# A three-stage kernel in fp32 split into halves: VectorE's and ScalarE's order in nine Strassen pairs of the channel mix is worked out by host code

## The chip, the cores and the metric

The kernel runs on one core of a Trainium2 chip. Times are device microseconds (us) of one execution. Beside the plain executions one was taken by the hardware profiler, and all rows below come from it. A core has TensorE (PE) for matmuls, VectorE (DVE), ScalarE (ACT), GpSimd (POOL, idle here) and SyncE (SP), which issues the transfers. Each engine has an instruction list of its own, and semaphores tie the lists together; in the trace every engine but PE's weight loads goes through its list in order.

## The reference

Three stages follow each other. The inputs are fp32.

```
scores = z @ z.T / S;  x = u * (relu(scores)**2 @ v)            # attention, 4 x 3072 x 256
x_prev = x shifted by one token
xk = mu_k*x + (1-mu_k)*x_prev;  xr = mu_r*x + (1-mu_r)*x_prev   # channel mix, 12288 tokens
x = sigmoid(xr @ w_r) * (relu(xk @ w_k)**2 @ w_v)               # 256 -> 1024 -> 256
out = relu(x @ w_in)**2 @ w_out                                 # MLP, 256 -> 2048 -> 256
```

## The kernel before

**Numbers.** A product of fp32 matrices is made of three matmuls of rounded numbers: an operand is cast to a high half (`hi`), and `lo = x - hi` holds the rest; `hi*hi`, `lo*hi` and `hi*lo` are added in PSUM. So each operand that comes out of a stage costs one cast and one subtraction. All matmuls of the mix and the MLP have 512 columns.

**Tiling.** The 12288 tokens are 24 blocks of 512. In the channel mix, blocks 0 to 5 go through plain matmuls. Blocks 6 to 23 go in nine pairs (`s` = 3 to 11) through a Strassen-Winograd form with seven products in place of eight; the MLP then takes the twelve pairs in the same form (`s` = 12 to 23). The change concerns the nine pairs of the mix.

**A round.** A pair of the mix has four rounds `(s, i)`, i = 0 to 3, each for two of the eight slices of the hidden layer. A round is written as units: `p0` to `p6` are the seven products (three matmuls each) into four PSUM banks, and `d0` to `d7` are the second layer's matmuls (three each) on the hidden tiles of the round before, in the order p0 d0 p1 d1 ... p6 d6 d7. Rounds 1 and 2 have two more units, `r0` and `r1`, of six matmuls each: the gate `xr @ w_r` of one block, into bank 1, which becomes `sig`. So a pair has 4 x 45 + 24 = 204 matmuls, and the nine have 1836.

**What VectorE and ScalarE do in a round.** ACT copies bank 0 (`p`, L916). DVE adds the banks up: `su` (bank 1), `sv` (bank 2), `s` for the hidden quarters 22, 12 and 21 (all L920). ACT makes relu and square (L925, L929), then a cast makes the high half (`hhi`, ACT L934 or DVE L936) and DVE the low half (`hlo`, L940). Bank 1 may be written again only when `su` has been made from it, bank 2 only after `sv`.

**What else they do in a pair.** The next pair's operands are prepared meanwhile: blocks of x are loaded (`load_x`, one buffer, x<-xT), blended on ACT and DVE (L191, L194) into the pair's `x2` tile, summed (`sums`, L851 to L855), and split into seven operands (`op_hi` L783, `op_lo` L787), which lie in nine buffers. The gate's operand `xr` is blended and split too (L798, L802). At a pair's end the two accumulators per block are multiplied by `sig` (`gate_v2`, L1029) and stored. Pieces of the MLP's weights are loaded and split (L711, L720).

**What sets the order.** All is under a manual schedule: an engine's order is the order in which the Python code emits. In the pairs of the mix a fixed table (`mix_tasks`) hangs each extra step on a unit, as `at(1, "p1", blend_r, n1, 0)`, and the steps of a round itself hang on units in one long if-chain. Scratch tiles come from rings in turn: `a` (4 tiles, p, v and the blends), `t` (6 tiles, the sums and hidden quarters), `h` (6 pairs of halves).

Of the kernel before, what the change touches and what calls it, by code (L numbers as in the profile page):

```python
# [23 lines left out]
def tile_relu2_attention__rwkv_channel_mix__relu2_mlp(  # L24
# [63 lines left out]

    def split(hi, lo, src, on_act=False):
        if on_act:  # L90
            nc.scalar.copy(hi, src)
        else:
            nc.vector.tensor_copy(hi, src)
        nc.vector.tensor_tensor(out=lo, in0=src, in1=hi, op=ALU.subtract)
# [93 lines left out]
    def blend(n, which, c, xm=None):  # L188
        t = x_t[n]
        m = el.tile([P, T], F32, tag="a", name="m")  # L190
        nc.scalar.activation(out=m, in_=t[:, c, 0:T], func=AF.Copy, scale=om[:, which, c:c + 1])  # L191
        if xm is None:
            xm = el.tile([P, T], F32, tag="a", name="xm")
        nc.vector.scalar_tensor_tensor(out=xm, in0=t[:, c, 1:], scalar=mu[:, which, c:c + 1], in1=m,  # L194
                                       op0=ALU.mult, op1=ALU.add)
        return xm
# [436 lines left out]
    def gate_v(n, d):  # L633
        t = hp.tile([P, T], F32, tag="t", name="xo", bufs=6)
        nc.vector.tensor_tensor(out=t, in0=acc_v[n][d], in1=sig.pop((n, d)), op=ALU.mult)
# [4 lines left out]
    def gate_r(n, d, xr, bank=None):  # L640
        ps = up(lambda h, c, f: wr[:, h, c, f * P:(f + 1) * P], xr, d, bank)
# [4 lines left out]
    def channel_mix():  # L646
# [25 lines left out]
        for f, *tasks in ((0, (stage_x, s, 1, 0), (wk_sums, 0, 0)), (1, (stage_x, s, 1, 1), (load_x, n0), (wk_sums, 0, 1)),  # L672
# [4 lines left out]
                           (load_x, n0 + 1), (load_wk, 1))):  # L677
# [25 lines left out]
    x2_raw, x2_tmp, ops, win, wout = {}, {}, {}, {}, {}  # L703
# [31 lines left out]
    def wk_split(h, g):  # L735
        i = 2 * h + g
        if h == 0:
# [6 lines left out]
        split(*ws[i], wk_total[h][1][:, g], True)  # L744
# [20 lines left out]
    def stage_x(s, b, c):  # L765
        if s not in x2_raw:
            x2_raw[s] = hp.tile([P, ND, 2 * T], F32, tag="x2", name="x2")
        blend(2 * s + b, 0, c, x2_raw[s][:, c, b * T:(b + 1) * T])
# [4 lines left out]
    def op_src(s, j):  # L773
        src = x2_raw[s].rearrange("x c (b t) -> x c b t", b=2)
        return (src[:, 0, 0], src[:, 0, 1], x2_tmp[s][:, 0] if s in x2_tmp else None, x2_tmp[s][:, 1], src[:, 1, 0],
                src[:, 1, 1], src[:, 1, 0])[j]

    def op_hi(s, j):
# [4 lines left out]
        nc.scalar.copy(ops[s, j][0], op_src(s, j))  # L783
# [10 lines left out]
    def blend_r(n, c):  # L794
        mixing[n, c] = blend(n, 1, c)

    def r_hi(n, c):
        nc.scalar.copy(xr_tile()[:, 0, c], mixing[n, c])  # L798
# [75 lines left out]
    def mlp():  # L874
# [39 lines left out]
        def first_sum(g):  # L914
            tmp[g, "p1"] = t = brief("p1")
            nc.scalar.copy(t, banks[g, 0])  # L916

        def add(g, to, bank, of):
            tmp[g, to] = t = (brief if to == "v" else scratch)("s" + to)
            nc.vector.tensor_tensor(out=t, in0=banks[g, bank], in1=tmp[g, of], op=ALU.add)  # L920

        def relu(g, c):
            if c == "11":
                tmp[g, c] = scratch("s11")
# [6 lines left out]
        def high(g, c):  # L931
            hi, lo = gt[g, c] = parts(hp, "h", 6)
            if c in ("22", "11") or (c == "12" and g[0] < NPAIR):
                nc.scalar.copy(hi, tmp[g, c])  # L934
            else:
                nc.vector.tensor_copy(hi, tmp[g, c])  # L936
# [60 lines left out]
        def side(g, stage):  # L997

            p, i = g
            if p < NPAIR:  # L1000
                return
# [30 lines left out]
        split_at = [(s, i) for s in range(PLAIN + 1, NPAIR) for i in (0, 1)][:12]  # L1032
        load_at = {(PLAIN, 3): 0, split_at[3]: 1, split_at[5]: 2, split_at[9]: 3}

        def mix_tasks(s):
            nxt, (n0, n1), (m0, m1) = s + 1, (2 * s, 2 * s + 1), (2 * s + 2, 2 * s + 3)
            more = nxt < NPAIR
            todo = {}

            def at(i, u, *a):  # L1040
                todo.setdefault((i, u), []).append(a)

            if s == PLAIN:
                at(0, "p1", op_hi, s, 4)
                at(0, "p1", op_lo, s, 4)
                at(0, "p1", op_hi, s, 5)
                at(0, "p1", sums, s, 2)
                at(0, "p1", op_lo, s, 5)
                at(0, "p2", op_hi, s, 6)
                at(0, "p2", op_lo, s, 6)  # L1050
                at(0, "p5", wk_sums, 1, 0)
                at(0, "p6", wk_sums, 1, 1)
                at(1, "p3", wk_split, 1, 0)
                at(1, "p4", wk_split, 1, 1)
            else:
                at(0, "p1", op_hi, s, 6)
                at(0, "p2", op_lo, s, 6)
            at(1, "p1", blend_r, n1, 0)
            at(1, "p2", blend_r, n1, 1)
            at(1, "r1", r_hi, n1, 0)  # L1060
            at(1, "r1", r_hi, n1, 1)
            at(1, "p5", r_lo, n1, 0)
            at(1, "p6", r_lo, n1, 1)
            if more:
                at(1, "p2", load_x, m1)
                at(1, "p6", stage_x, nxt, 1, 0)
                at(1, "d7", stage_x, nxt, 1, 1)
                at(1, "d7", load_x, m0)
                at(2, "p2", stage_x, nxt, 0, 0)
                at(2, "p3", stage_x, nxt, 0, 1)  # L1070
                at(2, "p5", blend_r, m0, 0)
                at(2, "p6", r_hi, m0, 0)
                at(2, "d7", r_lo, m0, 0)
                at(3, "p1", blend_r, m0, 1)
                at(3, "p1", load_x, m1)
                at(3, "p2", r_hi, m0, 1)
                at(3, "p3", r_lo, m0, 1)
            else:
# [161 lines left out]
```

## Time and profile before

| | |
|---|---|
| median of 3 runs | 2550.35 us (2545.96 to 2552.53) |
| profiled execution | 2551.01 us; its span, first to last instruction, 2549.1 us |
| PE busy | 2479.4 us, 97% of the span, 14745 matmuls |
| DVE, ACT busy | 2075.5 us (81%), 1830.8 us (72%) |
| mean granted clock of PE | 0.998 of full speed |

A busy PE in such a page is not PE at its peak, since matmuls overlap and their ends are modelled: a matmul of 512 columns shows some 389 ns, and the next may start earlier. What PE loses is therefore read from how far apart matmuls start.

### The profile page before, as it was taken

To read this page: it belongs to the slowest core of one execution; us is meant where nothing else is said; L and a number is where in the kernel's file an instruction comes from. 1 tells how busy PE (TensorE), PEld (TensorE's weight loads), DVE (VectorE), ACT (ScalarE), POOL (GpSimd) and SP (SyncE) were. 2 spreads that over 40 slices of the span, in tenths; PEclk is the share of its full clock that TensorE was granted. 3 is DMA by queue.
4 is the path that set the end of the run, shared out by engine and by line. 5 is a ranking of instruction groups with operands and counts; after the bars stand their busy time and mean duration, and the time that the engine had idled before them with its cause. 6 is when DMAs were issued, how large, how long until landed. Compare 5 with 4: busy or idle time off the path is not lost.

```text
span 2549.1 us, 39363 instructions
## 1 busy us (share of the span) xinstructions
PE 2479.4 (97%) x14745; PEld 2026.2 (79%) x14745; DVE 2075.5 (81%) x3431; ACT 1830.8 (72%) x3239; POOL 0.7 (0%) x6
## 2 busy tenths in 40 slices
PE   9999999999999999988888889999999999999999
PEld 6888898888888888766767667888888888888887
DVE  8998999889899868877788777877777777777776
ACT  8867876886797767777777776766666666666665
POOL 0000000000000000000000000000000000000000
PEclk9999999999999999999999999999999999999999
DMA  7686768757677633211111121001110011010100
GB/s 211 195 219 184 224 174 219 208 170 220 186 219 202 190 101 100 87 67 53 55 42 58 50 67 67 17 18 33 34 34 17 17 34 34 19 28 21 34 17 17
DMA packets 308895, 251.11 MB, mean 99 GB/s; under 512 B 205280, under 2 KB 224736, under 8 KB 305632
## 3 DMA queue, kind: packets, MB, share of 16 engines
q1 hardware_dynamic: 306592, 248.08, 33.3%
q8 instruction: 115, 1.88, 0.3%
q10 hardware_dynamic: 2112, 0.52, 0.1%
q14 instruction: 76, 0.62, 0.1%
HBM read 142.64 MB, written 105.91 MB: 98 GB/s over the span
## 4 chain that ended last, share of the span: by engine, by line
PE 75%; ACT 10%; DVE 9%; issue 3%; DMA 2%; DVEq 0%; SPq 0%; ACTq 0%
PE v L468 26%; PE ups L888 18%; PE v L904 7%; PE v L906 7%; PE v L905 7%; PE ups L224 4%; PE sps L430 3%; ACT s L925 2%; ACT s L929 2%; DVE s L920 2%; ACT a L391 1%; ACT hhi L934 1%; DVE hlo L940 1%; DMA x<-xT 1%; ACT a L434 1%
## 5 line engine op out<-in xcount | busy, mean ns | idle before, releaser
L468 PE MATMUL v<-ahi,vhl 64*128 64x512 f32 x4592 | 668.9, 387 | 0.0
L468 PEld LDWEIGHTS v<-ahi,vhl 64*128 64x128 f32 x4592 | 467.5, 184 | 88.8 <-ACT rest L478 3.7
L925 ACT ACTIVATE s<-s 128x512 f32<-128x512 f32 x396 | 248.9, 628 | 360.3 <-DVE s L920 359.2
L468 PE MATMUL v<-alo,vhl 64*128 64x512 f32 x2296 | 411.4, 386 | 0.6 <-DVE alo L444 0.5
L940 DVE TENSOR_TENSOR hlo<-s,hhi 128x512 fp32r<-128x512 f32 x528 | 363.3, 688 | 33.7 <-ACT hhi L934 17.0
L929 ACT ACTIVATE s<-s 128x512 f32<-128x512 f32 x528 | 318.0, 628 | 8.4
L920 DVE TENSOR_TENSOR s<-ups,su 128x512 f32<-128x512 f32 x264 | 180.7, 684 | 149.4 <-PE ups L888 149.4
L904 PE MATMUL v<-hhi,wout 128*128 128x512 f32 x768 | 299.5, 390 | 0.6 <-ACT hhi L934 0.6
L905 PE MATMUL v<-hhi,wout 128*128 128x512 f32 x768 | 299.1, 389 | 0.0
L906 PE MATMUL v<-hlo,wout 128*128 128x512 f32 x768 | 299.0, 389 | 0.0
L888 PE MATMUL ups<-d,win 128*128 128x512 f32 x1056 | 296.7, 389 | 0.0
L468 PEld LDWEIGHTS v<-alo,vhl 64*128 64x128 f32 x2296 | 250.9, 184 | 44.6 <-DVE alo L444 1.0
L888 PEld LDWEIGHTS ups<-d,win 128*128 128x128 f32 x1056 | 198.2, 188 | 41.2
L888 PE MATMUL ups<-b,win 128*128 128x512 f32 x792 | 222.5, 389 | 0.0
L444 DVE TENSOR_TENSOR alo<-a,ahi 128x512 fp32r<-128x512 f32 x334 | 219.4, 660 | 0.0
L434 ACT ACTIVATE a<-a 128x512 f32<-128x512 f32 x334 | 211.4, 633 | 10.3
L371 DVE STREAM_TRANSPOSE turn<-a 128x512 f32<-128x512 f32 x240 | 206.6, 861 | 13.4 <-ACT a L434 11.4
L391 ACT ACTIVATE a<-sps 128x512 f32<-128x512 f32 x335 | 197.5, 590 | 18.7 <-PE sps L430 16.8
L888 PEld LDWEIGHTS ups<-b,win 128*128 128x128 f32 x792 | 148.7, 188 | 30.9
L934 ACT CAST hhi<-s 128x512 fp32r<-128x512 f32 x300 | 171.5, 616 | 1.1
L904 PEld LDWEIGHTS v<-hhi,wout 128*128 128x128 f32 x768 | 144.4, 188 | 31.7 <-ACT hhi L934 1.0
L906 PEld LDWEIGHTS v<-hlo,wout 128*128 128x128 f32 x768 | 144.3, 188 | 29.9 <-DVE hlo L940 0.2
(168 smaller groups left out, 3904.0 us busy)
## 6 DMA issues: line engine op xcount, KB each, us to landing
turned<-turn SPq DMA_DIRECT2D x60, 1024.0 KB, 5.1
mixed<-turned SPq DMA_DIRECT2D x220, 256.0 KB, 5.0
x<-xT SPq DMA_DIRECT2D x29, 513.0 KB, 3.8
u<-in_u_dram SPq DMA_DIRECT2D x192, 64.0 KB, 3.6
xT<-uT SPq DMA_DIRECT2D x48, 256.0 KB, 2.6
x<-x2d SPq DMA_DIRECT2D x12, 1024.0 KB, 4.7
out_dram<-y SPq DMA_DIRECT2D x94, 128.0 KB, 2.3
raw<-in_v_dram SPq DMA_DIRECT2D x23, 512.0 KB, 5.2
```

The lines of the kernel that those rows point to most:

```text
L391: nc.scalar.activation(out=a, in_=ps, func=AF.Relu, scale=1.0 / S)
L434: nc.scalar.activation(out=a, in_=a, func=AF.Square)
L444: finish(lambda: nc.vector.tensor_tensor(out=lo, in0=a, in1=hi, op=ALU.subtract))
L468: nc.tensor.matmul(acc[n, d][i], lhsT=vt[rows, k % 2, c, ds_], rhs=at[s][k // 2][rows], start=first and k == 0, stop=last and k == 2)
L888: nc.tensor.matmul(ps, lhsT=weight(g, h, w), rhs=ops[g[0], j][y], start=first and m == 0, stop=m == 2, skip_group_check=not first)
L904: nc.tensor.matmul(acc[p, b][d], lhsT=w[:, 0, c, ds_], rhs=hi, start=first, stop=False)
L905: nc.tensor.matmul(acc[p, b][d], lhsT=w[:, 1, c, ds_], rhs=hi, start=False, stop=False)
L906: nc.tensor.matmul(acc[p, b][d], lhsT=w[:, 0, c, ds_], rhs=lo, start=False, stop=last)
L920: nc.vector.tensor_tensor(out=t, in0=banks[g, bank], in1=tmp[g, of], op=ALU.add)
L925: nc.scalar.activation(out=tmp[g, c], in_=banks[g, 0] if c == "11" else tmp[g, c], func=AF.Relu, scale=1.0 if g[0] < NPAIR else HS)
L929: nc.scalar.activation(out=tmp[g, c], in_=tmp[g, c], func=AF.Square)
L940: nc.vector.tensor_tensor(out=lo, in0=tmp.pop((g, c)), in1=hi, op=ALU.subtract)
```

## The change

`mix_tasks` and the parts of the if-chain that served the mix are gone. A function `mix_groups` lists all steps of the nine pairs as nodes with a cost, the engines that may take them and what they depend on, gives each the time by which its earliest user on PE needs it (`due`), and then plays the nodes through with one clock per engine. At each turn it takes the engine that can start first, and there the step with the earliest due time among those that are ready. The code is then emitted in that order. Four things come with it.

- The casts of the hidden quarters, of the operands, of `xr` and of w_k's sums are marked `"SV"`: the engine that is free first takes them.
- A blend of ACT and DVE works in place: ACT writes its part where DVE's sum will stand, with no tile of its own for it.
- The tiles of the rings `a`, `t` and `h` are made once, and a step takes whichever is free in that play (`take`, `held_by`, `place`).
- PE's order changes in one thing: `r0` and `r1` stand after `d4` and `d6`, no longer after `d2` and `d4`.

```diff
     def gate_v(n, d):
-        t = hp.tile([P, T], F32, tag="t", name="xo", bufs=6)
-        nc.vector.tensor_tensor(out=t, in0=acc_v[n][d], in1=sig.pop((n, d)), op=ALU.mult)
+        r = sig.pop((n, d))
+        t = hp.tile([P, T], F32, tag="t", name="xo", bufs=6) if n < NP - 1 else r
...
-            at(1, "p1", blend_r, n1, 0)
-            at(1, "p2", blend_r, n1, 1)
...
-                at(1, "p2", load_x, m1)
-                at(1, "p6", stage_x, nxt, 1, 0)
...
+            def either(f, *a, deps=(), due=1e9):
+                return node("SV", {"S": 0.525, "V": 0.36}, lambda e: f(*a, e == "S"), *deps, due=due)
...
+            def load(f, *a, deps=()):
+                return node("D", 3.5, lambda e: f(*a), *deps)
...
+            def gate_operand(n, *deps):
+                done = []
+                for c in range(ND):
+                    xm = use(blended(n, 1, c, *deps), ("xr", n, c))
+                    hi = use(either(r_hi, n, c, deps=(xm,)), ("xr", n, c))
+                    last["xr", n, c] = use(on_v(r_lo, n, c, deps=(hi,)), ("xr", n, c))
+                    done.append(xm)
+                return done
...
+                if i in (1, 2):
+                    for d in range(ND):
+                        r = on_pe(gate_unit, n, d, cost=1.36, deps=(last["bank", 1], *(last["xr", n, c] for c in range(ND))))
+                        last["bank", 1] = on_s(lambda n=n, d=d: gate_sig(n, d, gate_ps.pop((n, d))), deps=(r,))
+                        if d == 0:
+                            p = prod(5, v)
...
+                if i == 1:
+                    xs = gate_operand(n0 + 1, last["r", n0])
+                    clear = [last["op", s, j] for j in (1, 5, 6)]
+                    if nxt < NPAIR:
+                        last["x", m0 + 1] = load(load_x, m0 + 1, deps=xs)
+                        b1 = [blended(m0 + 1, 0, c, *clear) for c in range(ND)]
+                        last["x", m0] = load(load_x, m0, deps=b1)
+                        b0 = [blended(m0, 0, c, *clear) for c in range(ND)]
+                        staged = b0 + b1
...
+                    i = min((i for i, t in cand.items() if t <= start), key=lambda i: (nodes[i][4], i))
+                    if best is None or start < best[0]:
+                        best = start, e, i
```

PE, the second round of pair 7 (`v` are the second layer's accumulators, `mixed,wr` is the gate). Before, a `d2`, then `r0`, then `p3`:

```order
L904 MATMUL v_17162<-hhi,wv 128x512
L905 MATMUL v_17162<-hhi,wv 128x512
L906 MATMUL v_17162<-hlo,wv 128x512
L224 MATMUL ups<-mixed,wr 128x512 x6
L888 MATMUL ups<-u_15185,wse 128x512
L888 MATMUL ups<-u_15185,wsm 128x512
```

Now at the same gate, from `d3` on:

```order
L939 MATMUL v_16862<-hhi,wv 128x512
L940 MATMUL v_16862<-hhi,wv 128x512
L941 MATMUL v_16862<-hlo,wv 128x512
L923 MATMUL ups<-u_15196,wk 128x512 x3
L939 MATMUL v_16837<-hhi,wv 128x512
L940 MATMUL v_16837<-hhi,wv 128x512
L941 MATMUL v_16837<-hlo,wv 128x512
L230 MATMUL ups<-mixed,wr 128x512 x6
L923 MATMUL ups<-u_15221,wse 128x512
```

The gate's six matmuls moved behind `p3`, `d3`, `p4` and `d4`, four units of three matmuls.

VectorE at the turn from the first to the second round of the same pair. Before (`s_17106` is the quarter 21 of the first round, `su` and `sv` are the second round's):

```order
L920 TENSOR_TENSOR s_17106<-ups,su 128x512
L940 TENSOR_TENSOR hlo<-s_17072,hhi 128x512
L1029 TENSOR_TENSOR sig<-v_16700,sig 128x512
L1029 TENSOR_TENSOR sig<-v_16701,sig 128x512
L940 TENSOR_TENSOR hlo<-s_17088,hhi 128x512
L936 CAST hhi<-s_17106 128x512
L940 TENSOR_TENSOR hlo<-s_17106,hhi 128x512
L920 TENSOR_TENSOR su<-ups,p_17126 128x512
L194 SCALAR_TENSOR_TENSOR xm<-x,mu,m 128x512
L920 TENSOR_TENSOR sv<-ups,su 128x512
```

Now (tiles are called `st` and `sa` whatever they hold: the first row is the quarter 21, the rows with `st<-ups,sa`, `sa<-ups,st` are the second round's `su` and `sv`):

```order
L955 TENSOR_TENSOR st<-ups,st 128x512
L200 SCALAR_TENSOR_TENSOR st<-x,mu,st 128x512 x2
L972 TENSOR_TENSOR hlo<-st,hhi 128x512
L837 TENSOR_TENSOR mixed<-st,mixed 128x512
L955 TENSOR_TENSOR st<-ups,sa 128x512
L837 TENSOR_TENSOR mixed<-st,mixed 128x512
L955 TENSOR_TENSOR sa<-ups,st 128x512
L972 TENSOR_TENSOR hlo<-st,hhi 128x512
L955 TENSOR_TENSOR st<-ups,sa 128x512
```

The gate multiplies (L1029, now L1059) moved ahead of the quarter 21, and the low halves of the first round's last quarters moved behind `su` and `sv`; the gate's blends stand before them.

In the nine pairs 51 casts moved from ScalarE to VectorE: 38 of the 144 hidden ones, 10 of the 70 of operands, 2 of `xr` and 1 of w_k's sums. All other instructions keep their engine and their number.

## Rows read from the trace of the kernel before

**Rows 1.** Busy time by stretch: attention, the nine pairs, MLP.

```profile
core 0: us, PE busy (x) PEld busy (x) DVE busy (x) ACT busy (x) POOL busy (x), PEclk, DMA share, GB/s
200.00:400.00 200.00, 199.57 (x1754) 169.31 (x1754) 182.06 (x306) 156.31 (x277) 0.00 (x0) 1.00 0.72 203
1063.03:1554.08 491.05, 436.23 (x1836) 341.73 (x1837) 381.41 (x621) 363.50 (x652) 0.00 (x0) 0.99 0.16 53
1640.00:2230.00 590.00, 590.00 (x2604) 488.35 (x2603) 446.19 (x716) 389.47 (x695) 0.00 (x0) 1.00 0.09 27
```

**Rows 2.** Busy time by pair (columns as before): 3, 7, 11.

```profile
1063.03:1123.96 60.93, 52.48 (x204) 39.49 (x205) 45.98 (x75) 41.87 (x75) 0.00 (x0) 0.94 0.17 60
...
1287.58:1341.81 54.23, 48.10 (x206) 37.75 (x204) 43.26 (x73) 40.44 (x74) 0.00 (x0) 1.00 0.15 49
...
1504.52:1554.08 49.56, 47.16 (x205) 37.99 (x204) 36.99 (x60) 36.69 (x67) 0.00 (x0) 1.00 0.12 43
```

**Rows 3.** Busy time by round (same columns): pair 3's first, pair 7's first three.

```profile
1063.03:1078.59 15.56, 13.36 (x46) 8.96 (x47) 11.60 (x18) 8.73 (x16) 0.00 (x0) 0.89 0.19 67
...
1287.58:1298.15 10.57, 10.57 (x46) 8.29 (x45) 9.13 (x17) 7.66 (x16) 0.00 (x0) 1.00 0.01 2
1298.15:1314.36 16.21, 13.48 (x58) 10.55 (x57) 12.74 (x23) 12.44 (x24) 0.00 (x0) 1.00 0.27 97
1314.36:1328.71 14.35, 13.21 (x58) 10.62 (x57) 9.95 (x15) 10.68 (x20) 0.00 (x0) 1.00 0.12 38
```

**Rows 4.** What PE waited for in the nine pairs (total us, times, longest).

```profile
PE ups L224 <- DVE su L920: 24.4, 17, 1.8
PE ups L888 <- DVE sv L920: 12.5, 9, 1.5
PE v L904 <- DVE sig L1029: 10.7, 8, 1.8
```

**Rows 5.** Timeline (start, duration; idle before and its releaser), pair 7's first gate unit.

```profile
1302.51 0.57 ACT L916 COPY p<-ups 128x512 f32<-128x512 f32 x1
...
1303.59 0.42 DVE L936 CAST hhi<-s 128x512 fp32r<-128x512 f32 x1
1304.04 0.69 DVE L940 TENSOR_TENSOR hlo<-s,hhi 128x512 fp32r<-128x512 f32 x1
1304.65 0.68 DVE L920 TENSOR_TENSOR su<-ups,p 128x512 f32<-128x512 f32 x1
...
1305.39 1.66 PE L224 MATMUL ups<-mixed,wr 128*128 128x512 f32 x6 [1.50 <-DVE su L920]
```

**Rows 6.** Timeline of VectorE: two gate multiplies back to back, merged.

```profile
1299.40 1.28 DVE L1029 TENSOR_TENSOR sig<-v,sig 128x512 f32<-128x512 f32 x2
```

**Rows 7.** Nine pairs by line and form (count | busy, mean ns | idle, releaser): VectorE, ScalarE.

```profile
L940 DVE TENSOR_TENSOR hlo<-s,hhi 128x512 fp32r<-128x512 f32 x141 | 96.7, 686 | 15.7 <-ACT hhi L934 14.4
L936 DVE CAST hhi<-s 128x512 fp32r<-128x512 f32 x35 | 14.7, 420 | 0.3 <-ACT s L929 0.3
L194 DVE SCALAR_TENSOR_TENSOR x<-x,mu,m 128x512 f32<-128x512 f32 x32 | 23.3, 748 | 15.9 <-ACT m L191 15.9
L851 DVE TENSOR_TENSOR d<-x 128x1024 f32<-128x1024 f32 x10 | 12.2, 1217 | 0.0
...
L929 ACT ACTIVATE s<-s 128x512 f32<-128x512 f32 x142 | 85.3, 626 | 2.2
L934 ACT CAST hhi<-s 128x512 fp32r<-128x512 f32 x107 | 62.4, 616 | 1.1
L191 ACT ACTIVATE m<-x,om 128x512 f32<-128x512 f32 x68 | 48.2, 720 | 40.4 <-DMA x<-xT 24.9 <-DVE su L920 15.5
```

**Rows 8.** The loads of x in the nine pairs: issue (ns) and landing.

```profile
L182 SPq DMA_DIRECT2D x<-xT x23: 359/370/371, 1069.8 to 1500.3; - x23
...
DMA to landing us min/median/max: 3.6/3.8/4.9
```

**Rows 9.** ScalarE's waits for these loads (total us, times, longest).

```profile
ACT m L191 <- DMA x<-xT: 24.9, 8, 3.2
```

## What the change will do to the time

> **What bounds the kernel now.** I read the busy time by stretch first. In the MLP 2604 matmuls take 590 us, so one every 0.2266 us, and VectorE is busy there for 446.19 of the 590; in the attention VectorE is busy 182.06 of 200 and PE still 199.57 [rows 1]. Neither stretch is touched. The nine Strassen pairs of the mix are different: 1836 matmuls, which at 0.2266 us each would fill 416.0 us, take 491.05 us [rows 1]. So PE loses 75.0 us there, 2.9% of the kernel, and none of the other engines is full: VectorE has 381.41 busy, ScalarE 363.50, and the transfers use 0.16 of the DMA engines. All that the change can win lies in these 75.0 us.
>
> Where are they? A pair has 204 matmuls, 46.2 us at full pace. Pair 3 takes 60.93 us and pair 11 takes 49.56 [rows 2]; the seven between take together 491.05 - 60.93 - 49.56 = 380.6, 54.4 each, of which pair 7 is one. So the losses are 14.7, 7 times 8.1, and 3.3 us. Within pair 7 the first round has 10.57 us where 45 matmuls need 10.20; the second has 16.21 and the third 14.35 where 57 need 12.92 [rows 3]. The loss sits in the rounds with gate units and with most of the preparation for the next pair; pair 11, which prepares no blocks for a next one, loses least.
>
> The list of waits names what PE stood for: 24.4 us in 17 waits of the gate's first matmul for `su`, 12.5 us for `sv`, 10.7 us for the gate multiplies, each at most 1.8 us [rows 4]. The timeline shows one. ScalarE's copy, from which `su` is made, ended at 1302.51 + 0.57 = 1303.08. VectorE began `su` only at 1304.65, because a cast and a low half of the round before stood ahead of it, and PE, free since about 1303.9, began the gate at 1305.39 [rows 5]. What stood ahead was due much later: it is the quarter 21, which PE takes in `d6` only, 33 matmuls or 7.5 us on. So these are waits of order on VectorE, not of work.
>
> **The change, part by part.**
>
> *The gate units go four units back.* Four units of three matmuls are 12 x 0.2266 = 2.72 us. The gate in pair 7 would have been free to start at 1303.9; its `su` was ready at 1305.39. Moved by 2.72 it starts no earlier than 1306.6, and the wait is covered with 1.2 us to spare even if `su` came no sooner. So I take the 24.4 us of `su` as gone. What this costs: the block's `xr` is read 2.72 us later, and the next block's blends, which now wait for that, start the chain of loads later (below).
>
> *VectorE's order.* In the row order of the change the multiplies of the gate come ahead of the quarter 21, and two low halves and a cast go behind `su` and `sv`. But two blends, a low half and a gate low half now stand between the quarter 21 and `su`: 2 x 0.748 + 2 x 0.686 = 2.87 us, against 4 x 0.686 + 0.68 + 0.42 = 3.84 before [rows 6, 7]. So `su` does not come first, only sooner by about 1 us; the slack of the moved gate is what covers it. I count the 12.5 us for `sv` and 10.7 for the gate as gone too, since each single wait is at most 1.8 us.
>
> *51 casts change engine.* ScalarE loses 51 x 0.616 = 31.4 us of its 363.50, VectorE gains 51 x 0.420 = 21.4 us on its 381.41 [rows 1, 7], which makes 402.8. Against PE's 416.0 this is 0.97, and the attention has PE full only beside a VectorE of 0.91 [rows 1]. If 0.91 is as much as VectorE can be filled, the nine pairs need 402.8 / 0.91 = 442.6 us. If it can be filled wholly, PE's pace is the floor. Back to back the next instruction starts earlier than the durations say: two multiplies take 1.28 us together, 0.08 less than 2 x 0.68 [rows 6], so a fuller VectorE also counts fewer busy microseconds, and 402.8 is an upper reading.
>
> [...]
>
> *In-place blends, scratch tiles given out once, gate_v in place.* No instruction is added, and a blend reads and writes as many elements as in its row of 0.748 us [rows 7]; the gate multiplies already work in place, at the usual pace [rows 6]. I cost them at 0; below nothing they could go only by a tile that came free sooner, and no wait in rows 4 is for a tile. If a tile is given out that is free in the plan but not yet on the chip, a wait comes in; that is the last rival.
>
> *The loads.* Per pair two loads of x stand in series between blends (`load_x` of m0+1, then m0), and the plan counts 3.5 us for each. The trace has 3.8 from issue to landing (up to 4.9), and issuing takes SyncE 0.36 [rows 8]; so each comes 0.66 us later than planned, 1.3 per pair. In SyncE's list a load can also stand behind a store that waits for its gate multiply, 0.68 us. Behind a late load ScalarE's blend waits, and behind that, on ScalarE, the next round's copy and relus; VectorE and PE wait for those. The whole chain from a pair's last `xr` read in round 1 to the next pair's first product is: three steps of blending at 2 x 0.72 + 0.75 = 2.2, two loads at 4.2, the sums 1.22, a cast 0.62 and a low half 0.69, together 17.5 us, with 0.7 + 12.9 + 10.2 = 23.8 us between. The 6.3 us over are spread on some eleven links, so about one foreign instruction ahead of each uses them up. I therefore let the 1.3 us through to PE in full, 9 x 1.3 = 11.7 us; 0 is its lower end, and its upper end is a rival.
>
> *The MLP's weight pieces* come in single steps, spread over later rounds, in place of blocks of two or four steps; they are as many instructions as before, due only in the MLP, and I cost them at 0 with the rest of VectorE's load, which 402.8 holds.
>
> *The start of pair 3.* Its first round takes 15.56 us, 5.4 over its 10.20, with the granted clock at 0.89 [rows 3]: PE falls for a part of it from the 2.4 to the 1.2 GHz level after it stood still. The operands it waits for come from the code ahead, which keeps its order but for one load. I leave 5.4 us standing. The 9.3 us that pair 3 loses in its other rounds go as in the other pairs.
>
> **Sum.** 416.0 + 5.4 + 11.7 = 433.1 us for the nine pairs, against 491.05: 58.0 us less. The profiled execution took 2551.0 us (2549.1 of span and 1.9 around it), so 2493.0; it stands 0.7 us from the median of the runs, which is nothing here. Ends for this case: 416.0 + 5.4 = 421.4, which gives 2481.4, and 442.6, with the start 448, which gives 2508. I predict 2493 us, 2.3% faster.
>
> **The rivals.**
>
> *VectorE becomes the bound.* If every one of its 621 + 51 instructions kept its full duration, 0.08 us would be added to 621 of them: 381.4 + 49.7 + 21.4 = 452.5 us, and with the start 458, so 2518 us. For it: 0.97 is higher than any stretch here shows beside a full PE. Against it: the overlap in rows 6.
>
> *The loads bind.* ScalarE's waits for x are 24.9 us in 8, 3.1 each [rows 9]. If each of the two loads of a pair held PE for 3.1 us: 416.0 + 5.4 + 18 x 3.1 = 477 us, so 2537. Against it: eight such waits in nine pairs reach PE now only in part.
>
> *The gaps are for want of banks.* Four PSUM banks serve as before, and each wait in rows 4 is for one to be read out. If the bank, not the order, sets the gap, it moves and does not shrink: 2551 us, no change. Against it: in rows 5 the bank's reader had its input 1.57 us before it began. The Trainium skill, page "Perfetto Trace Analysis", section "Identifying Performance Opportunities", says that the same gap repeating on the engine that should be full can mean too few buffers in SBUF or PSUM; by that rule this rival would hold, and the timeline of rows 5 disagrees.
>
> *Slower: the six scratch tiles lock the engines in step.* The `t` tiles now also hold the gate's blends, and each is reused as soon as the plan has it free. If in each of the 36 rounds PE had to wait for one whole chain from a bank to a low half, add, relu, square, cast, low half, 2 x 0.686 + 2 x 0.626 + 0.616 = 3.2 us [rows 7], that is 116 us: 416.0 + 5.4 + 116 = 538, so 2598 us. It ends above the kernel before once a round loses more than (491.05 - 421.4) / 36 = 1.9 us. Against it: a hidden quarter now has most of a round from its sum to its matmul.
>
> **Chances.** Forecast (2481 to 2508) 0.67, VectorE the bound (to 2523) 0.12, loads 0.07, no change 0.06, slower 0.08. The first two make the range, 2480 to 2523, with 0.79. A difference within 0.3% (7.7 us) can't be told from none; of the cases the first three are faster by more, 0.86, the fourth is the same, 0.06, the last slower, 0.08.
>
> **What would show it.** Right: pairs of 47 to 48 us between the first and the last; waits of the gate for `su` near zero; VectorE busy at 0.90 or more of the nine pairs, near 400 us; pair 3's first round still near 15 us; attention and MLP unmoved. Wrong by VectorE: pairs near 50 us, PE waiting for `su`, `sv` and low halves in all rounds, VectorE without idle time. Wrong by loads: waits of ScalarE for x in most pairs, and first products of a pair late. Wrong by tiles: VectorE and ScalarE both idle in every round, each waiting for the other.

## The result, and the profile after

The changed kernel takes 2479.19 us (median of 4 runs, 2478.77 to 2480.53) against 2548.35 us before in the same comparison (4 runs): a ratio of 0.9728, interval 0.9711 to 0.9745, so 2.7% faster. The forecast was 2493.0 us with a range from 2480 to 2523; the kernel came out 13.8 us below the one and 0.8 us below the other. The profiled execution has a span of 2477.4 us, 71.7 us less than before.

First the windows of the changed kernel, in one fence: attention, the nine pairs and the MLP; pairs 3, 4, 7 and 11; the first round of pair 3, and the first and the second of pair 7; the MLP's second and third round.

```profile
core 0: us, PE busy (x) PEld busy (x) DVE busy (x) ACT busy (x) POOL busy (x), PEclk, DMA share, GB/s
200.00:400.00 200.00, 199.56 (x1754) 170.75 (x1752) 181.89 (x306) 155.97 (x276) 0.00 (x0) 1.00 0.72 202
1062.08:1485.61 423.53, 420.55 (x1837) 344.68 (x1837) 395.30 (x676) 341.37 (x604) 0.00 (x0) 1.00 0.18 61
1600.00:2200.00 600.00, 600.00 (x2648) 496.64 (x2647) 454.67 (x729) 395.90 (x705) 0.00 (x0) 1.00 0.09 25
...
1062.08:1114.89 52.81, 49.89 (x204) 38.78 (x205) 49.06 (x89) 36.58 (x68) 0.00 (x0) 0.97 0.18 60
1114.89:1161.81 46.92, 46.86 (x205) 37.98 (x204) 44.65 (x77) 40.51 (x73) 0.00 (x0) 1.00 0.19 68
1254.41:1300.65 46.24, 46.24 (x205) 38.29 (x204) 41.92 (x71) 39.13 (x71) 0.00 (x0) 1.00 0.17 58
1439.37:1485.61 46.24, 46.24 (x206) 38.29 (x204) 44.68 (x76) 35.22 (x62) 0.00 (x0) 1.00 0.18 62
...
1062.08:1078.29 16.21, 13.53 (x45) 9.01 (x46) 14.08 (x26) 7.60 (x14) 0.00 (x0) 0.89 0.19 65
1254.41:1264.61 10.20, 10.20 (x46) 8.45 (x45) 10.20 (x19) 8.85 (x17) 0.00 (x0) 1.00 0.00 0
1264.61:1277.53 12.92, 12.92 (x58) 10.70 (x57) 12.44 (x22) 10.66 (x19) 0.00 (x0) 1.00 0.35 124
...
1495.81:1506.01 10.20, 10.20 (x47) 8.45 (x45) 8.75 (x17) 4.18 (x9) 0.00 (x0) 1.00 0.62 206
1506.01:1517.22 11.21, 10.86 (x47) 8.21 (x46) 9.43 (x18) 8.80 (x18) 0.00 (x0) 1.00 0.16 54
```

Set against [rows 1 to 3], the attention and the MLP's long stretch have a full PE as before, and the nine pairs take 423.53 us instead of 491.05: 67.5 us less. Pair 7 takes 46.24 us where it took 54.23, and that is 204 matmuls at 0.2267 us, the full pace. Pair 11 has the same length; so have all from 7 on. What is left over nine times 46.24 = 416.2 us is 7.4 us: 6.6 in pair 3, 0.7 in pair 4, 0.1 in pairs 5 and 6.

Next what PE still waits for in the nine pairs (total us, times, longest), and below it ScalarE's waits for the loads of x.

```profile
PE ups L923 <- ACT u L90: 2.9, 2, 2.3
PE ups L923 <- DVE sa L955: 1.1, 1, 1.1
PE ups L923 <- DVE u L817: 0.8, 1, 0.8
PE v L941 <- DVE hlo L972: 0.2, 1, 0.2
...
ACT x L191 <- DMA x<-xT: 5.8, 8, 2.3
```

The 47.6 us of waits for `su`, `sv` and the gate's multiplies [rows 4] are gone, and what stands there belongs mostly to pair 3's start (the wait of 2.3 us lies ahead of its first product). ScalarE waits 5.8 us for x instead of 24.9 [rows 9]. The same gate unit as in [rows 5], in the changed kernel's timeline (`su` is now an `st` tile made from `sa`), and below it a wait of PE in the same round of the kernel before:

```profile
1270.00 0.68 DVE L955 TENSOR_TENSOR st<-ups,sa 128x512 f32<-128x512 f32 x1
...
1271.41 1.52 PE L230 MATMUL ups<-mixed,wr 128*128 128x512 f32 x6
```

```profile
1300.22 0.47 PE L904 MATMUL v<-hhi,wv 128*128 128x512 f32 x1 [1.23 <-DVE sig L1029]
```

The sum now begins 5.39 us after its round's start (1264.61); before it was 1304.65 - 1298.15 = 6.50. But 1.23 us of these 6.50 PE itself stood still, for a gate multiply; without them it is 5.27, so against PE's pace `su` is no sooner here. What has moved is the gate: ahead of it stand ten units of three matmuls, 6.80 us, where six stood before, 4.08 us at full pace. So `su` ends 0.73 us before PE comes to the gate.

The work itself by line (count | busy, mean ns | idle before): there are 73 hidden casts on VectorE where [rows 7] have 35, and the operations cost what they cost.

```profile
L972 DVE TENSOR_TENSOR hlo<-st,hhi 128x512 fp32r<-128x512 f32 x142 | 96.4, 683 | 4.4 <-ACT hhi L90 3.3
L90 DVE CAST hhi<-st 128x512 fp32r<-128x512 f32 x73 | 30.5, 421 | 5.2 <-ACT st L964 4.8
```

**Where the 71.7 us are.** 67.5 in the nine pairs. The MLP's second and third rounds took 11.84 and 12.76 us before; now 10.20 and 11.21, so 3.2 us. And the first product of pair 3 stands at 1062.08 instead of 1063.03, 0.95 us, with the same order ahead of it but for one load. The two rows of the kernel before that show the MLP's part are its second and third round:

```profile
1564.28:1576.12 11.84, 10.51 (x46) 8.18 (x44) 9.30 (x18) 4.44 (x10) 0.00 (x0) 1.00 0.52 179
1576.12:1588.88 12.76, 12.17 (x45) 9.58 (x46) 10.70 (x21) 10.31 (x20) 0.00 (x0) 0.87 0.23 74
```

### The profile page after: what moved, and what is told of

The parts are those of the page before. It is cut to its first block, busy times and chain, and to the rows that moved or that the text cites. A ratio compares the mean times of both kernels' runs of the same rounds, so it can differ in the third digit from the quotient of the medians.

```text
span 2477.4 us, 39355 instructions
## 1 busy us (share of the span) xinstructions
PE 2461.8 (99%) x14745; PEld 2061.4 (83%) x14745; DVE 2086.6 (84%) x3482; ACT 1807.0 (73%) x3188; POOL 0.7 (0%) x6
## 4 chain that ended last, share of the span: by engine, by line
PE 89%; ACT 4%; DVE 4%; issue 2%; DMA 1%; SPq 1%; DVEq 0%; ACTq 0%
PE v L474 26%; PE ups L923 24%; PE v L941 9%; PE v L939 9%; PE v L940 9%; PE ups L230 5%; PE sps L436 3%; ACT a L397 1%; ACT a L440 1%; PE v L256 1%; PE v L252 1%; PE v L253 1%; DVE alo L450 0%; ACT vhl L343 0%; DVE turn L377 0%
## 5 line engine op out<-in xcount | busy, mean ns | idle before, releaser
L474 PE MATMUL v<-ahi,vhl 64*128 64x512 f32 x4592 | 676.5, 387 | 0.0
L474 PEld LDWEIGHTS v<-ahi,vhl 64*128 64x128 f32 x4592 | 488.6, 184 | 68.7 <-ACT rest L484 3.7
L474 PE MATMUL v<-alo,vhl 64*128 64x512 f32 x2296 | 418.7, 386 | 0.1
L960 ACT ACTIVATE s<-s 128x512 f32<-128x512 f32 x288 | 181.2, 629 | 320.1 <-DVE s L955 320.1
L474 PEld LDWEIGHTS v<-alo,vhl 64*128 64x128 f32 x2296 | 262.3, 184 | 33.5 <-DVE alo L450 0.5
L972 DVE TENSOR_TENSOR hlo<-s,hhi 128x512 fp32r<-128x512 f32 x384 | 264.5, 689 | 18.0 <-ACT hhi L90 2.7
L964 ACT ACTIVATE s<-s 128x512 f32<-128x512 f32 x384 | 231.4, 628 | 6.1
L955 DVE TENSOR_TENSOR s<-ups,su 128x512 f32<-128x512 f32 x192 | 131.4, 684 | 121.9 <-PE ups L923 121.9
L939 PEld LDWEIGHTS v<-hhi,wout 128*128 128x128 f32 x768 | 144.1, 188 | 31.5 <-ACT hhi L90 0.8
L940 PEld LDWEIGHTS v<-hhi,wout 128*128 128x128 f32 x768 | 144.2, 188 | 29.3
```

Source lines behind the costliest of these rows:

```text
L474: nc.tensor.matmul(acc[n, d][i], lhsT=vt[rows, k % 2, c, ds_], rhs=at[s][k // 2][rows], start=first and k == 0, stop=last and k == 2)
L939: nc.tensor.matmul(acc[p, b][d], lhsT=w[:, 0, c, ds_], rhs=hi, start=first, stop=False)
L940: nc.tensor.matmul(acc[p, b][d], lhsT=w[:, 1, c, ds_], rhs=hi, start=False, stop=False)
L960: nc.scalar.activation(out=tmp[g, c], in_=banks[g, 0] if c == "11" else tmp[g, c], func=AF.Relu, scale=1.0 if g[0] < NPAIR else HS)
L964: nc.scalar.activation(out=tmp[g, c], in_=tmp[g, c], func=AF.Square)
L972: nc.vector.tensor_tensor(out=lo, in0=tmp.pop((g, c)), in1=hi, op=ALU.subtract)
```

## The experiments

The theory to test: the order in which VectorE and ScalarE take their work is the whole gain. Rivals: the moved gate units bring it, or the free choice of the casts' engine; or a wait that is removed only moves on to the next thing that is late. One rival was not tried: that blends in place and freely given tiles bring a part of it. Then a second question: why late loads, to which the forecast gave 11.7 us, cost nothing. The times of runs without an interval are single ones.

**The gate moved alone, in the kernel before.** The gate units stand behind `d4` and `d6`, and a cast and the low halves of the gate's operands hang later with them; everything else is as before.

```diff
-            at(1, "p5", r_lo, n1, 0)
-            at(1, "p6", r_lo, n1, 1)
+            at(1, "d7", r_lo, n1, 0)
+            at(1, "d7", r_lo, n1, 1)
...
-                at(2, "p6", r_hi, m0, 0)
+                at(2, "d7", r_hi, m0, 0)
...
-                    if mixed and k in (2, 4):
-                        gate_r(2 * g[0] + g[1] - 1, k // 4, xr_tile(), 1)
...
+                    if mixed and k in (4, 6):
+                        gate_r(2 * g[0] + g[1] - 1, (k - 4) // 2, xr_tile(), 1)
...
```

> The kernel before with one part of the change alone: the gate units r0 and r1 stand after d4 and d6, with the gate's casts and low halves hung behind r1; the table of steps is otherwise kept. Theory A (the order on VectorE and ScalarE is what counts, the moved gate covers only its own waits): the 24.4 us of waits of the gate for su go, but some come back at the next bank or at the low halves behind it; nine pairs 460 to 475 us of 491.05, 2525 to 2535 us in all. Theory B (the moved gate is most of the change): nine pairs under 440 us, under 2505 us. Theory C (the waits only move on to the next bank): 485 us or more, no change.

Measured: ratio 1.0005, interval 0.9995 to 1.0014; nine pairs 493.1 us. PE's three largest waits in them:

```profile
PE ups L224 <- ACT sig L644: 31.4, 17, 2.6
PE ups L888 <- ACT sig L644: 12.2, 9, 1.9
PE v L904 <- DVE sig L1029: 8.2, 7, 1.7
```

The 24.4 us for `su` are gone from the list, and 31.4 us for the sigmoid that empties a bank stand in their place, 17 times again. Moved alone, in a table that is otherwise not planned around it, the gate only finds the next thing that is late.

**The gate moved back, in the changed kernel.** Its units stand behind `d2` and `d4` again, and the order is planned anew around them.

```diff
+                if i in (1, 2):
+                    gate(0)
                 p = prod(3, get("bank", 3))
...
                 if i in (1, 2):
...
+                    gate(1)
+                p = prod(5, v)
...
```

> The changed kernel with the gate units put back behind d2 and d4; the order by need, the free choice of engine and the tiles stay, and the plan is worked out anew. Theory A: the order by need brings su in time by itself, so the nine pairs lose at most 1 us each, 424 to 433 us against 423.5 of the changed kernel. Theory B: 10 us or more come back in rounds 1 and 2, waits of the gate for su above 10 us.

Measured: 2480.06 us, nine pairs 423.9 us, PE's waits for `su` 0.4 us in all. The second round of pair 7, from its first product to the gate:

```profile
1265.14 0.84 PE L923 MATMUL ups<-u,wk 128*128 128x512 f32 x3
...
1267.85 0.69 DVE L955 TENSOR_TENSOR st<-ups,sa 128x512 f32<-128x512 f32 x1
...
1269.22 1.52 PE L230 MATMUL ups<-mixed,wr 128*128 128x512 f32 x6
```

Here `su` begins 2.71 us into its round, half of the 5.39 above, and is again done 0.68 us ahead of the gate. So the plan brings `su` as soon as its reader needs it, and the gate's place is worth nothing once the order is planned: that rival falls.

**The casts tied to their engines.** In the changed kernel each cast is given to ScalarE, but for those of the quarter 21, which VectorE had before.

```diff
-                return node("SV", {"S": 0.525, "V": 0.36}, lambda e: f(*a, e == "S"), *deps, due=due)
+                e = "V" if f is high and a[1] == "21" else "S"
+                return node(e, {"S": 0.525, "V": 0.36}[e], lambda e: f(*a, e == "S"), *deps, due=due)
```

> The changed kernel with every cast tied to the engine that it had before (36 hidden casts on VectorE, all others on ScalarE). VectorE then has some 21 us less and ScalarE 31 us more, both under the 416.0 us of PE. Theory A (order, not load): nine pairs 423 to 428 us, no difference beyond 0.3%. Theory C (the choice of engine is needed): 435 us or more, with PE waiting for halves whose casts stand late on ScalarE.

Measured: 2480.6 us. Its nine pairs:

```profile
1060.99:1486.77 425.78, 422.24 (x1836) 345.99 (x1837) 377.13 (x624) 355.89 (x653) 0.00 (x0) 0.99 0.18 60
```

VectorE has 18 us less and ScalarE 15 more than in the changed kernel, and PE's loss grows by 2.3 us, of which 1.8 are pair 3's. The choice of engine is not the gain either.

**Played in the written order.** The host plays the same steps by the same costs, but of two steps that could start it takes the one written first, not the one due first.

```diff
-                    i = min((i for i, t in cand.items() if t <= start), key=lambda i: (nodes[i][4], i))
+                    i = min((i for i, t in cand.items() if t <= start), key=lambda i: i)
```

> The changed kernel with one word of the plan changed: among the steps that are ready an engine takes the one that is written first, not the one that is due first. Due times are still worked out but unused. Theory A (earliest need): steps of a later round can't overtake, but preparation written behind its round is held up less than the round's own; pairs of 47 to 52 us, nine pairs 435 to 465 us. Rival (any order in which no engine waits for a step that is not ready is as good): 423 to 428 us.

Measured: 2514.64 us, nine pairs 457.1 us; a middle pair takes 48.8 to 49.2 us, and the loss sits in its last round. The timeline of VectorE there, pair 7, with PE's wait below it:

```profile
1313.69 1.22 DVE L886 TENSOR_TENSOR d<-x 128x1024 f32<-128x1024 f32 x1
...
1318.56 1.29 DVE L837 TENSOR_TENSOR mixed<-st,mixed 128x512 fp32r<-128x512 f32 x2
1319.76 0.68 DVE L955 TENSOR_TENSOR st<-ups,sa 128x512 f32<-128x512 f32 x1
1320.36 0.68 DVE L817 TENSOR_TENSOR u<-d,u 128x512 fp32r<-128x512 f32 x1
1320.96 0.68 DVE L955 TENSOR_TENSOR sa<-ups,st 128x512 f32<-128x512 f32 x1
...
1321.70 0.96 PE L923 MATMUL ups<-u,mixed 128*128 128x512 f32 x3 [1.75 <-DVE sa L955]
```

Sums, low halves and blends for the next pair run without a gap ahead of `u` (`st<-ups,sa`), and another low half ahead of `v` (`sa<-ups,st`); PE stands for that `v` nine times, 19.0 us in all. The changed kernel has the same stretch in this order:

```profile
1293.19 0.68 DVE L955 TENSOR_TENSOR st<-ups,sa 128x512 f32<-128x512 f32 x1
...
1294.12 1.22 DVE L886 TENSOR_TENSOR d<-x 128x1024 f32<-128x1024 f32 x1
1295.26 0.68 DVE L955 TENSOR_TENSOR sa<-ups,st 128x512 f32<-128x512 f32 x1
1295.86 0.68 DVE L972 TENSOR_TENSOR hlo<-st,hhi 128x512 fp32r<-128x512 f32 x1
1296.45 0.68 DVE L955 TENSOR_TENSOR st<-ups,sa 128x512 f32<-128x512 f32 x1
```

`u` stands ahead of the sums `d`, `v` right behind them. So of the 67.5 us the choice by earliest need is worth 33.5, of which 10.5 belong to pair 3 (63.3 us here, 52.8 in the changed kernel). The other 34 come from playing the steps by when they can start, together with all else in the change. Blends in place and tiles given out freely are in these 34, and no run has them apart. That they count for something is possible: in [rows 7] ScalarE's blends wait 15.5 us for `su`. By the program such a blend reads only x, so what it waits for is the tile of ring `a` that `su` frees; in the changed kernel its blends wait for loads alone.

**All casts on VectorE.** What if VectorE is fuller still?

```diff
-                return node("SV", {"S": 0.525, "V": 0.36}, lambda e: f(*a, e == "S"), *deps, due=due)
+                return node("V", 0.36, lambda e: f(*a, e == "S"), *deps, due=due)
```

> The changed kernel with all casts of the nine pairs tied to VectorE, so 165 more than the plan gave it. VectorE then has 395 us busy and 165 casts at 0.36 us back to back to 0.42 alone, 455 to 465 us, and is the bound, above the 416.0 us of PE. If VectorE can be filled wholly under this planner: nine pairs 460 to 470 us, VectorE busy above 0.97 of it. If 0.91 to 0.93 is as much as it can be filled: 490 to 510 us.

Measured: 2512.96 us. Nine pairs, then the second round of pair 8:

```profile
1061.74:1518.77 457.03, 430.67 (x1837) 342.34 (x1838) 443.35 (x831) 257.54 (x446) 0.00 (x0) 1.00 0.17 56
...
1328.72:1344.04 15.32, 13.79 (x59) 10.51 (x57) 15.32 (x30) 8.81 (x15) 0.00 (x0) 1.00 0.29 104
```

VectorE is busy 443.35 of 457.03 us, 0.97, and 15.32 of 15.32 in that round. A limit of 0.91, one end of the forecast, is refuted.

**Later loads.** In two variants of the changed kernel SyncE issues a second transfer into the same tile behind each load of x, which the plan does not know of: a 64 KB piece of it, or the whole load again.

```diff
...
-                return node("D", 3.5, lambda e: f(*a), *deps)
+                return node("D", 3.5, lambda e: [f(*a), again(*a) if f is load_x else None], *deps)
```

> The changed kernel with a second, small transfer (64 KB, a part of the same x into the same place) behind each load of x in the nine pairs; the plan still counts 3.5 us for both. Each x comes some 2 us later, as the smallest stores here take 2.0 us, so 4 us per pair. By the prediction's step (the chain of blends and loads has no room left, a late load goes through to PE in full): 8 pairs x 4 = 32 us more, nine pairs 455 us. By the theory formed from the trace of the changed kernel (low halves of a pair's first operands end 1.2 to 2.5 us before their product, and ScalarE waited for x only 5.8 us in 8 waits): most of it is hidden, 425 to 440 us.

> The changed kernel with each load of x in the nine pairs done twice, one behind the other; the plan is the same. Each x comes some 4.2 us later, 8.4 us per pair. Prediction's step, no room: 8 x 8.4 = 67 us more, 490 us. Some 2 us of room per load: 8 x 4.4 = 35 us, 455 to 465 us. Hidden wholly: under 430 us.

Measured: 2505.49 us with nine pairs of 449.3, and 2536.93 us with 481.0. ScalarE's waits for x, of the piece and of the whole load:

```profile
ACT x L191 <- DMA x<-xT: 33.8, 16, 5.5
```

```profile
ACT x L191 <- DMA x<-xT: 63.6, 16, 6.4
```

Eight pairs have 16 such loads. A load makes ScalarE wait 5.8 / 16 = 0.36 us in the changed kernel, 2.1 with the piece and 4.0 with the whole load again; a load then costs (449.3 - 423.5) / 16 = 1.6 and (481.0 - 423.5) / 16 = 3.6 us. The difference is 0.4 to 0.5 us each time: in this order so much of a wait is free, on average, and the rest goes through to PE. Both runs lie nearer to what the prediction's step gives, 455 and 490, than to the theory formed after the result, by which most of the piece would be hidden (425 to 440).

**The plan without its allowances.** The host counts 0.3 us from PE's end to the start of who waits for it, and 0.15 us from VectorE's or ScalarE's. First these are cut, and then the load is counted at 4.2 us besides.

```diff
-            LAG = {"P": 0.3, "V": 0.15, "S": 0.15, "D": 0.0}
+            LAG = {"P": 0.1, "V": 0.0, "S": 0.0, "D": 0.0}
```

> The changed kernel, but the plan's allowance between the end of one instruction and the start of the next engine's is taken down from 0.3 us (TensorE) and 0.15 us (VectorE, ScalarE) to 0.1 and 0.0 us; every instruction stays. The question is why loads of x that land 0.2 to 1.2 us later than the plan's 3.5 us cost nothing in pairs 7 to 11. Theory M: the plan's other allowances are longer than the chip's, and they cover the late loads; without them the order is planned too tight, and each pair loses 0.5 to 1.5 us: nine pairs 428 to 436 us against 423.5. Rival S: the order itself has slack behind the loads whatever the plan assumed; nine pairs 423 to 425 us.

> As the run without allowances, but the plan counts 4.2 us for a load where it counted 3.5. Theory M: what the loads lack is given back; of the loss against the changed kernel at least half is gone again, nine pairs 423.5 to 430 us. If the loss stays as it was without allowances, the loads are not what the allowances covered. Rival S: 423 to 425 us again, as without allowances.

Measured: 2513.17 us with nine pairs of 456.7, and 2507.41 us with 451.2. Two waits of the first, then the same two of the second:

```profile
ACT x L191 <- DMA x<-xT: 24.0, 8, 4.1
PE ups L923 <- ACT sig L656: 19.3, 17, 2.3
```

```profile
PE ups L923 <- ACT sig L656: 14.7, 18, 1.3
...
ACT x L191 <- DMA x<-xT: 0.6, 1, 0.6
```

The loss, 33.2 us, is far over the 5 to 12 that I expected, and mostly it is not the loads': counted rightly they make ScalarE wait 23.4 us less, and the pairs take only 5.5 us less. Of the 27.7 us that stay, 14.7 are PE's waits for the gate's sigmoid to empty a bank. So the allowances cover other hand-overs more than the loads, this one above all; what the other 13.0 us are was not taken apart. Theory M was right on the sign and wrong on what they cover.

**The doubled load, told to the plan.** The whole load again, and the plan counts 8.0 us for it.

> The changed kernel with each load of x issued twice, as in the run that did so before (nine pairs 481.0 us), but the plan now counts 8.0 us for a load. If the loss of that run came from an order planned for the wrong time, most of it goes: nine pairs 425 to 440 us. If the chain of two loads and four blends is simply too long, its length decides: the prediction's 17.5 us and two loads longer by about 4.3 us each are 26.1 us in a stretch of 23.8 us, so at least 2.3 us lost in each of eight pairs, 18 us in all, and with what the plan's links lose beyond it 440 to 470 us.

Measured: 2509.34 us with nine pairs of 453.7, so 27.3 us of the 57.5 come back. The first round of a middle pair, then the pair:

```profile
1318.80:1331.66 12.86, 11.36 (x46) 8.15 (x45) 12.86 (x23) 11.90 (x22) 0.00 (x0) 1.00 0.02 10
...
1318.80:1367.89 49.09, 47.59 (x205) 37.91 (x204) 41.89 (x71) 38.63 (x70) 0.00 (x0) 1.00 0.26 86
```

The pair loses 2.85 us, nearly all of it in its first round, where its operands come late. The prediction's chain, two loads longer by 4.3 us, is 26.1 us in 23.8: 2.3 us too long. That fits, but it is not shown to be the cause: the nine pairs lose from 2.3 to 5.5 us each, and in the round above VectorE has no gap either (12.86 of 12.86 us). What is shown is that a plan hides the chain without the longer loads.

**Pair 3's start earlier.** First all preparation hangs one step of the plain blocks earlier; then both blends of its first half side by side, and sums and operands behind them earlier too.

```diff
-                at(NP - 1, f, *task)
+                at(NP - 1, max(0, f - 1), *task)
```

> The changed kernel with the steps that prepare pair 3 (blends, sums and the first four operands, hung on the last plain block) moved one step of the plain block ahead, some 2.7 us. Pair 3's first round loses 6.0 us in the changed kernel, and PE waits 2.3 us for its first product. If these operands are late by order: 2 to 5 us less, 2474 to 2477 us. If the load of x behind them is what is late: no change, 2479.

```diff
...
-                          (2, (wk_split, 0, 0), (wk_split, 0, 1)), (3, (stage_x, s, 0, 0)),
-                          (4, (stage_x, s, 0, 1), (sums, s, 0)), (5, (op_hi, s, 0), (op_lo, s, 0), (sums, s, 1), (op_hi, s, 1)),
...
+                          (1, (wk_split, 0, 0), (wk_split, 0, 1)), (2, (stage_x, s, 0, 0), (stage_x, s, 0, 1)),
+                          (3, (sums, s, 0), (op_hi, s, 0), (op_lo, s, 0)), (4, (sums, s, 1), (op_hi, s, 1), (op_lo, s, 1)),
...
```

> The changed kernel with the work ahead of pair 3 hung earlier: both blends of its first half hang two steps of the plain blocks earlier side by side, then sums, high and low parts a step or two earlier each. If the wait at pair 3's start is a matter of this order alone, TensorE's waits for u there (2.3 and 0.8 us) fall under 0.5 us each and the first round falls from 16.2 us to 13.5 to 14.5 us, the kernel by 1.5 to 3.5 us (2476 to 2478 us). Rival: the blend still waits for the load of x, which can't leave earlier, or ScalarE's work for the last plain blocks now stands behind the blends and TensorE waits there instead: within 1 us of the changed kernel's 2479.2 us.

Measured: 2480.52 us (ratio to the kernel before 0.9731, interval 0.9715 to 0.9747) and 2481.79 us (0.9733, 0.9719 to 0.9746): neither beats the changed kernel. The first round of pair 3 in the second:

```profile
1062.83:1080.52 17.69, 12.80 (x45) 7.78 (x46) 14.77 (x27) 9.77 (x18) 0.00 (x0) 1.00 0.18 59
```

PE's wait ahead of the first product falls from 2.25 to 0.29 us, and yet the round begins no sooner, since PE ends the last plain blocks later (1062.54 against 1059.83); it then waits 1.1 us twice inside the round. The round ends at 1080.5 us; at 1078.3 in the changed kernel and in the first variant, and at 1078.6 before. So a shorter wait ahead of the first product did not bring that end forward; what would is open.

## Why the prediction was wrong

The mechanism was forecast rightly in the main, and two terms failed. The 11.7 us for the loads were 0: most of the distance to 2493. And the MLP, put at nothing, gave 3.2 us: this took the time below the range, since the nine pairs with 423.5 us lie between the forecast's ends for them (421.4 and 448). By its own steps:

- *All that can be won lies in the 75.0 us, and the waits there are of order, not of work*: right within the pairs. The written order costs 33.5 us with the same work, and pairs at the floor with VectorE busy 395.3 of 423.5 us are only to be had if work was not the limit. Not all of the gain lies there, though: see the MLP below.
- *The moved gate covers the 24.4 us for `su`*: so it does in the gate unit above, with 0.73 us to spare, but it isn't needed. Alone it turns the waits into 31.4 us for the sigmoid; put back in the changed kernel it costs nothing, since the plan then brings `su` 2.7 us sooner. *`su` sooner by about 1 us*: not in that unit. The 1.1 us that the rows seem to show are PE's own stand of 1.23 us in the round before the change, so the match is luck.
- *VectorE*: 402.8 us forecast as an upper reading, 395.3 measured, 0.93 of the stretch. The rival that makes it the bound (2518 us) is refuted. The Trainium skill, page "VectorE: DVE Perf Modes", section "The DRAIN you can't avoid", says that the next operation does not start until the pipe has emptied, and adds that one which is not held back starts earlier. The timeline above agrees with what it adds: VectorE's additions and subtractions of 0.68 us begin 0.60 us apart (1295.26, 1295.86, 1296.45).
- *Blends in place and scratch tiles, cost 0, since no wait in rows 4 is for a tile*: rows 4 list PE's waits alone. ScalarE's 15.5 us for `su` in [rows 7] are, by the program, waits for a tile, and they are gone. Whether PE gained by it is open.
- *The loads, 11.7 us*: the step that failed for the time. "The 6.3 us over are spread on some eleven links, so about one foreign instruction ahead of each uses them up. I therefore let the 1.3 us through to PE in full". Pairs 7 to 11 show 0.0 us of it. In the changed kernel's order a late load goes through, but only beyond 0.4 to 0.5 us, and the wait that a load really causes is 0.36 us, not the 0.66 by which it exceeds the plan's 3.5: for half of the 16 loads ScalarE is not yet at the blend when the load lands (8 waits). The row to read was how long ScalarE waits for a load in an order that is planned around it, and no run of the kernel before has one; the lower end 0 was the right one.
- *The start, 5.4 us*: 6.0 in the first round, and 1.4 us more in pair 3's second round and pairs 4 to 6. Sized nearly right.
- *Neither stretch besides is touched*: the step that failed for the range, by 3.2 us in the MLP's second and third rounds. Before, PE waits there 1.3 us for a relu and 0.6 for a cast of ScalarE, and after these waits the mean granted clock of the third round is 0.87, so a part of it runs at 1.2 GHz in place of 2.4; now the one wait left is 0.4 us and the clock stays at 1.00. What the relu stands behind on ScalarE is a piece of the MLP's weights. Its issue, its cast and PE's wait before, then its issue and cast now:

```profile
1567.90 1.60 SPq L100 DMA_DIRECT2D raw<-w_in  x1
...
1574.04 1.02 ACT L711 CAST win<-raw 128x256 fp32r<-128x256 f32 x3 [6.53 <-DMA raw<-w_in]
...
1576.13 0.96 PE L888 MATMUL ups<-u,win 128*128 128x512 f32 x3 [1.34 <-ACT s L925]
```

```profile
1498.79 0.45 SPq L100 DMA_DIRECT2D raw<-w_in  x1
...
1503.57 1.02 ACT L723 CAST win<-raw 128x256 fp32r<-128x256 f32 x3 [5.17 <-DMA raw<-w_in]
```

The cast begins 9.76 us into the second round before (1564.28) and 7.76 now (1495.81): the issue is 0.64 us sooner in its round, and from there to the cast it takes 4.78 us instead of 6.14. Why it takes less is open. All twelve kernels with a planned order have these rounds at 10.20 and 11.0 to 11.5 us, also the one played in the written order (10.20 and 11.28); the one with only the gate moved has 11.28 and 12.87. So it was none of the gate's place, the casts' engine and the choice by need that removed it.

- *No change, for want of banks*: the same four banks serve, and the loss fell from 75 to 7 us. By the page "Perfetto Trace Analysis" of the Trainium skill, section "Identifying Performance Opportunities", the same gap over and over can mean too few buffers; here the banks stayed four, and the gaps went with the order of their readers. *Slower, by tiles in lock-step*: no trace of it, and in the pairs from 7 on PE has no wait at all.

The sum with what was measured: 423.5 us for the nine pairs instead of 433.1, so 9.6 us of the 13.8 (11.7 less for the loads, 2.0 more for the start, 0.1 more for the floor); 3.2 us of the MLP; and 0.95 us by which the pairs began sooner. The last is scatter: in all runs of this document the pairs begin between 1060.99 and 1063.82. Without the MLP's 3.2 us the kernel would have stood at 2482.4, inside the range; its lower end held nothing outside the nine pairs.

## What to carry to other kernels

Where PE has short waits for engines that are not full, put the work of these engines in the order of need before moving work between them. Here the planned order, with the tiles freed for it, gave 67.5 us, at least 33.5 of them by the choice of the step due first; the gate's place and the casts' engine gave a few microseconds at most. A planned order is as good as the times it is planned with, and here it paid that they err on the long side at the hand-overs: taking 0.15 to 0.2 us off each cost 33 us. Ask of a late transfer how long its reader really waits and not how late it is; and look behind the changed stretch too, at the first rounds of the next one.

## What was not expected of the hardware

VectorE can be kept busy for 0.97 of 457 us beside PE and ScalarE, with 831 instructions, and for the whole of single rounds of 10 to 15 us. In the changed kernel PE runs without any gap beside a VectorE of 0.91 (41.92 of 46.24 us in pair 7) to 0.97 (44.68 in pair 11), and in pair 7's first round beside one that is busy all of its 10.20 us.
